# Layer norm, windowed attention and a gated unit on one core: the next chunk's rows are turned earlier, and other transfers change places

## The chip, the cores and the metric

The kernel runs on one core of a Trainium2 chip. A core has a matrix engine (TensorE, PE in the profile, with PEld for its weight loads), a vector engine (VectorE, DVE), a scalar engine (ScalarE, ACT), GpSimd (POOL) and a queue engine (SyncE, SP). Transfers between the chip's memory (DRAM) and the on-core memory are issued by an engine's queue, and run on 16 DMA engines that all queues share. The metric is the device time of one execution in microseconds; less is better.

## The reference

The input x has 2048 rows of 640 numbers. All numbers are bfloat16.

```python
xn = layernorm(x)                                  # rows: (x - mean) / sqrt(var + 1e-5)
q, k, v = split(xn @ wqkv)                         # 32 heads of 20 each
p = softmax(mask(q @ k.T * 20 ** -0.5))            # row i sees columns i-255 ... i
a = (p @ v) @ wo
b = (sigmoid(xn @ w_gate) * (xn @ w_up)) @ w_down  # 640 -> 1536 -> 640
out = x + a + b
```

`setup_inputs` also draws a `B_x`, which the reference does not use.

## The kernel before

The 2048 rows are worked in four chunks of 512 (c = 0 to 3), and each chunk in four blocks of 128 rows (s). Per chunk:

- **Rows.** `load_x` (L115) brings the chunk's x rows with four transfers into the tile `xc`, of which there is one buffer for all chunks. VectorE makes mean and variance of a block (`ln_block`, L214 and L220), POOL the inverse roots of all four blocks (`rstd_blocks`, L228 and L229), VectorE the normalized rows (`norm_rows`, L233). For chunks 1 to 3 the rows are then turned into columns in two halves: VectorE turns 32x32 squares (`turn_block`, L250), and `turn_rows` writes the result to DRAM with one transfer (L255) and reads it back in another order with four (L257) as `xnT`. Chunk 0 uses TensorE transposes instead.
- **Q and K.** `g_qk` has ten blocks of five matmuls (`proj_block`, L272): five of Q, copied out of PSUM by VectorE (L276), and five of K, copied by ScalarE (L278). Each copy is a tile `st`, one of six, which SP stores (L280) into a DRAM scratch, `sq` or `sk`. There a head has 32 rows, of which 20 are data; the other 12 are written once with zeros by `clear` (L153). `spread` (L290) reads the scratch back, one transfer for a pair of head groups, into `qT` and `kT`, where the scores read them. A chunk has four pairs (r = 0 to 3).
- **V.** `g_v` (L323): eight groups of ten short matmuls, copied by VectorE and ScalarE (L327).
- **Gate and up.** `g_gu` runs blocks of 128 of the 1536 hidden columns, twelve per chunk: five matmuls for the gate (L409), a tanh on ScalarE (L412), five matmuls for up (L416), and a product on VectorE (L420). The weights are loaded in eight transfers (`load_gu`, L156): the tiles `wg` and `wu` have two parts of 768 columns, each loaded in two halves of 384, so that a half serves three blocks.
- **Scores and P·V.** Chunk 0 has 16 score steps, the others 20. A step is 16 or 24 small matmuls (L492), one exponential on ScalarE (L498), masks on POOL (L481) and on VectorE (L509). Two steps after a pair's last score step its P·V follows (`pv`, L525), then VectorE turns and scales the result (L536 to L559).
- **Output.** `g_out`: down-projection (L430) and W_o (L437) into the same PSUM tile, VectorE adds x (L441), SP stores. `load_wd` (L176) loads W_down with five transfers; `turn_wo` (L185) reorders W_o in DRAM with eight transfers and `load_wo` (L190) loads the result.

The order of instructions on every engine is that of the program text; nothing is rescheduled. In front of the score steps and between them a queue of work called `fill` gives out matmul blocks: parts with names (`gu0a`, `gu0b`, `qk1`, `v1`, `gu0c`, and so on) that run in the order in which they were added, each with a cost in nanoseconds that says how much of it goes between two score steps. `mix(a, b, first, every)` takes a block of `a` and then a step of `b`, from block number `first` on. So steps for VectorE, such as statistics and turns, stand between the matmul blocks. Six half-blocks of gate and up run before the first score step; a chunk's first score step waits in the text for the whole of its `qk` part.

All matmul outputs but the scores go through four PSUM banks in rotation (`ps_d`); the scores have one tile of four banks. SP's transfers use eight semaphores in turn, so a transfer is issued once the eighth before it has landed.

Of the kernel before, what the change touches and what calls it, by code (L numbers as in the profile page):

```python
# [9 lines left out]
P = 128  # L10
# [5 lines left out]
DC = D // P  # L16
# [3 lines left out]
SBC = CW // P  # L20
# [5 lines left out]
FS = 768  # L26
# [10 lines left out]
FP32 = mybir.dt.float32  # L37
# [8 lines left out]
NP = NG // 2  # L46
# [20 lines left out]
def kernel(  # L67
# [11 lines left out]
    nc = tc.nc  # L79
    x2 = A_x.flatten_outer_dims()  # L80
# [3 lines left out]
    def pool(name, bufs, **kw):  # L84
        return ctx.enter_context(tc.tile_pool(name=name, bufs=bufs, **kw))
# [3 lines left out]
    lnp = pool("lnp", 4)  # L89
# [20 lines left out]
    def load_x(c):  # L110
        t = xp.tile([P, SBC, D], BF16, name="xc")
        xc[c] = t
        rows = x2[c * CW:(c + 1) * CW, :].rearrange("(a n t) d -> a t n d", a=SBC, n=SBC)
        for a in range(SBC):
            nc.sync.dma_start(out=t[32 * a:32 * a + 32], in_=rows[a])  # L115
# [3 lines left out]
    wg = [const.tile([P, DC, FS], BF16, name=f"wg{k}") for k in range(F // FS)]  # L119
    wu = [const.tile([P, DC, FS], BF16, name=f"wu{k}") for k in range(F // FS)]  # L120
# [30 lines left out]
    def clear(w):  # L151
        rows = scratch[w].rearrange("(h j) s -> h (j s)", j=32)[:, DH * CW:]
        nc.sync.dma_start(out=rows.rearrange("h (a e) -> h a e", a=4), in_=zero[:, 0:3, :])  # L153

    def load_gu(t, w, k, lo=0, hi=FS):
        nc.sync.dma_start(out=t[k][:, :, lo:hi],  # L156
                          in_=w.rearrange("(c p) f -> p c f", p=P)[:, :, k * FS + lo:k * FS + hi])

    load_gu(wg, B_w_gate, 0, 0, FS // 2)
    load_gu(wu, B_w_up, 0, 0, FS // 2)  # L160
    clear("q")
    clear("k")
    load_gu(wg, B_w_gate, 0, FS // 2)

    def load_rest():
        load_gu(wg, B_w_gate, 1, 0, FS // 2)
        load_gu(wu, B_w_up, 1, 0, FS // 2)
        load_gu(wg, B_w_gate, 1, FS // 2)
        load_gu(wu, B_w_up, 1, FS // 2)
        spread("q", 0, 2, NP)  # L170
        spread("k", 0, 2, NP)

    def load_wd():
        wd_r = B_w_down.rearrange("(c p) d -> p c d", p=P)
# [3 lines left out]
    wo_i = tc.dram_tile([HG, NG * DH, D], BF16, name="wo_i")  # L178
# [32 lines left out]
    def ln_half(c, s, a, stats=None):  # L211
        if a == 0:
            stats = lnp.tile([P, 2, nc.vector.BN_STATS_DIM], FP32, name="stats")
        nc.vector.bn_stats(out=stats[:, a, :], in_=xc[c][:, s, a * HALF:(a + 1) * HALF])  # L214
        return stats

    def ln_mv(stats, mv=None):
        if mv is None:
            mv = lnp.tile([P, nc.vector.BN_AGGR_DIM], FP32, name="mv")
        nc.vector.bn_aggr(out=mv, in_=stats)  # L220
        return mv

    def ln_block(c, s, mv=None):
        return ln_mv(ln_half(c, s, 1, ln_half(c, s, 0)), mv)

    def rstd_blocks(mvs):
        rstds = lnp.tile([P, SBC], FP32, name="rstds", bufs=1)
        nc.gpsimd.tensor_scalar(out=rstds, in0=mvs[:, :, 1], scalar1=EPS, scalar2=None, op0=ADD)  # L228
        nc.gpsimd.tensor_tensor(out=rstds, in0=rstds, in1=neghalf, op=POW)  # L229
        return rstds  # L230
# [13 lines left out]
    def turn_block(c, s):  # L244

        if s == 0:
            turns[c] = lnp.tile([P, SBC * D], BF16, name="turn", bufs=1)
        out_v = turns[c].rearrange("p (g m n t) -> p n g m t", g=HG, m=DC, n=SBC)
        in_v = xc[c][:, s, :].rearrange("p (m g j) -> p g m j", g=HG, m=DC)
        nc.vector.transpose(out=out_v[:, s], in_=in_v)  # L250

    def turn_rows(c):
        xnT[c] = xtp.tile([P, SBC, DC, P], BF16, name="xnT")
        rows = tc.dram_tile([HG, P, D], BF16, name=f"turn{c}")
        nc.sync.dma_start(out=rows.rearrange("g p e -> p g e"), in_=turns[c].rearrange("p (g e) -> p g e", g=HG))  # L255
        for g in range(HG):
            nc.sync.dma_start(out=xnT[c][32 * g:32 * g + 32].rearrange("p a m t -> p a (m t)"),  # L257
                              in_=rows[g].rearrange("(a j) e -> j a e", j=32))
# [3 lines left out]
    qk = {}  # L262
# [16 lines left out]
        dst = scratch[w].rearrange("(h j) s -> h j s", j=32)  # L279
        nc.sync.dma_start(out=dst[:, 4 * m:4 * m + 4, :], in_=st)  # L280

    def spread(w, c, r0, r1):

        half, first = divmod(r0, NP // 2)
        if first == 0:
            qk[w, c, half] = (qp if w == "q" else kp).tile([P, GH, CW], BF16, name=w + "T")
        src = scratch[w].rearrange("(a r p) s -> p r a s", a=2, p=P)
        to = qk[w, c, half].rearrange("p (r a) s -> p r a s", a=2)
        for r in range(r0, r1):
            nc.sync.dma_start(out=to[:, r % 2], in_=src[:, r])  # L290

    def new_v(c, s):
        v = vp.tile([P, 2, 16 * VW + 11], BF16, name="v")
# [35 lines left out]
    MM = 216  # L329

    def g_stats(c, out):


        mvs = lnp.tile([P, SBC, nc.vector.BN_AGGR_DIM], FP32, name="mvs", bufs=1)
        for s in range(SBC):
            ln_block(c, s, mvs[:, s, :])
            if s == SBC - 1:
                rstds = rstd_blocks(mvs)
            yield 0
        yield 0  # L340
        out.extend((mvs, rstds))

    def norm_rows(c, s, mvs, rstds):
        norm_block(c, s, mvs[:, s, :], rstds[:, s:s + 1], xc[c][:, s, :])
# [10 lines left out]
                turn_rows(c)  # L355
            yield 0

    def g_quick(c):
        got = []
        yield from g_stats(c, got)  # L360
        for s in range(0, SBC, 2):
            norm_rows(c, s, *got)
            norm_rows(c, s + 1, *got)
            yield 0
        for s in range(SBC):
            turn_block(c, s)
            if s == SBC - 1:
                turn_rows(c)
            yield 0

    def g_qk(c):
        for w in "qk":
            for m in range(DC):
                proj_block(w, c, m)
                if c == 0 and w == "q" and m == 1:
                    load_x(1)
                yield 5 * MM
        if c:
            spread("q", c, 0, 2)
            spread("k", c, 0, 2)  # L380
        else:
            for r in range(2):
                spread("q", c, r, r + 1)
                spread("k", c, r, r + 1)
                if r == 0:
                    load_gu(wu, B_w_up, 0, FS // 2)
# [14 lines left out]
    def part(w, d, f):  # L401
        k, first = divmod(f * P, FS)
        return w[k][:, d, first:first + P]

    def g_gu(c, f0, f1):
        for f in range(f0, f1):
            pg = ps_d.tile([P, CW], FP32, name="pg", tag="d")
            for d in range(DC):
                nc.tensor.matmul(pg, lhsT=part(wg, d, f), rhs=xnT[c][:, :, d, :],  # L409
                                 start=(d == 0), stop=(d == DC - 1))  # L410
            th = tp.tile([P, CW], FP32, name="th")
            nc.scalar.activation(out=th, in_=pg, func=TANH, scale=0.5)  # L412
            yield 5 * MM
            pu = ps_d.tile([P, CW], FP32, name="pu", tag="d")
            for d in range(DC):
                nc.tensor.matmul(pu, lhsT=part(wu, d, f), rhs=xnT[c][:, :, d, :],  # L416
                                 start=(d == 0), stop=(d == DC - 1))
            h = hp.tile([P, CW], BF16, name="h")
            ht[c, f] = h
            nc.vector.scalar_tensor_tensor(out=h, in0=th, scalar=1.0, in1=pu, op0=ADD, op1=MULT)  # L420
            yield 5 * MM
# [181 lines left out]
    def mix(a, b, first, every=1, rest=True):  # L603

        for k, cost in enumerate(a):
            yield cost
            if k >= first and (k - first) % every == 0:
                yield next(b, 0)
        if rest:
            yield from b  # L610
# [46 lines left out]
    r0 = root(mv0)  # L657
    r1 = root_act(1, xn1, neg1)
# [29 lines left out]
    nc.scalar.activation(out=scr, in_=neghalf[:, 0:1], func=EXP)  # L688
    banks.close()
    ps_s = banks.enter_context(tc.tile_pool(name="ps_s", bufs=1, space=bass.MemoryType.PSUM))  # L690
    for _ in g_qk(0):
        pass
    load_rest()

    fill = Fill()
    GU = 10 * MM
    OUT = 4 * 34 * 136
    APART = 1800
    def later(load, *args):
        load(*args)  # L700
        yield 0

    norms1 = g_quick(1)
    norms2 = itertools.chain(g_norms(2, True), later(load_x, 3))
    norms3 = g_norms(3, False)
    fill.add("gu0a", mix(g_gu(0, 0, 4), norms1, 0, 1, False), 4 * GU)
    fill.add("gu0b", mix(g_gu(0, 4, 10), norms1, 0), 6 * GU)
    fill.add("x2", later(load_x, 2), 0)
    fill.add("wo_i", later(turn_wo), 0)
    fill.add("qk1", g_qk(1), 50 * MM)  # L710
    fill.add("v1", mix(g_v(1), norms2, 2, 1, False), 40 * 136)
    fill.add("wd", later(load_wd), 0)
    fill.add("wo", later(load_wo), 0)
    fill.add("gu0c", mix(g_gu(0, 10, 12), norms2, 0, 1, False), 2 * GU)
    fill.add("gu1a", mix(g_gu(1, 0, 2), norms2, 0, 1, False), 2 * GU)
    fill.add("out0", mix(g_out(0, g_gu(1, 2, 3)), norms2, 1, 1), OUT + GU)
    fill.add("qk2", mix(g_qk(2), norms3, 2, 1, False), 50 * MM)
# [43 lines left out]
    c = NCH - 1  # L761
# [64 lines left out]
```

## Time and profile before

| | |
|---|---|
| median of three runs | 311.09 us (310.32 to 311.52) |
| the profiled execution | 311.1 us, its span 309.4 us |
| busy: PE, PEld, DVE, ACT, POOL | 303.5, 168.0, 187.2, 192.6, 79.1 us |
| granted TensorE clock | 1.00 throughout |
| moved by DMA | 36.86 MB, mean 119 GB/s |
| first Q matmul of chunk 0, of chunk 1 | 13.27 us, 51.27 us |
| first score step | 30.62 us |
| first matmul of the down-projection | 84.41 us |

The span is cut from the first to the last instruction of one profiled execution; its own time is 1.7 us longer. Times in the trace count from the start of the span. A row of a timeline has start, duration of the group, engine, line, operation, output and input, count, and in brackets the idle time before it with what ended it. For a transfer the row on a queue (SPq) is its issue; the time until its data has landed is a number of its own ("us to landing"). Busy times of PE overlap a little, since matmuls are pipelined, so a stall shows in the starts of the groups rather than in their sum.

### The profile page before, as it was taken

Reading aid. Unit: us, or ns where it says so; the run is one execution under the profiler, and the core shown is the slowest. Engines: PE = TensorE matmul, PEld = TensorE weight load, DVE = VectorE, ACT = ScalarE, POOL = GpSimd, SP = SyncE. Lnnn points to the kernel's source line nnn. Section 1 sums busy time; section 2 is a strip of 40 time slices with the busy share of each in tenths; the row PEclk is TensorE's granted clock in tenths of the full one; section 3 lists DMA queues with packets and bytes.
Section 4 is the critical chain, followed back from the end, with each engine's and each line's share of the span. In section 5 each row is a group of like instructions: output and inputs, shape, how many; then the busy total and the mean of one; then the engine's idle time right before and its main releaser. Section 6 shows DMA issues by size and latency. Waiting matters only on the chain.

```text
span 309.4 us, 10124 instructions
## 1 busy us (share of the span) xinstructions
PE 303.5 (98%) x4431; PEld 168.0 (54%) x4431; DVE 187.2 (61%) x372; ACT 192.6 (62%) x184; POOL 79.1 (26%) x172
## 2 busy tenths in 40 slices
PE   7999998999999999999999999999999999999996
PEld 3654443565456655644556655653445665444775
DVE  4736858659894679667653657346383627474423
ACT  6923875797674566869574656877676466768100
POOL 5000423133423123521223132331313232231100
PEclk9999999999999999999999999999999999999999
DMA  7987967549916722540251212560000110000301
GB/s 212 364 292 214 334 214 209 172 131 287 289 45 178 168 91 90 176 135 0 89 127 49 61 58 88 152 218 2 2 2 2 58 53 23 2 2 2 87 22 64
DMA packets 36140, 36.86 MB, mean 119 GB/s; under 512 B 2944, under 2 KB 35840, under 8 KB 36096
## 3 DMA queue, kind: packets, MB, share of 16 engines
q1 hardware_dynamic: 35232, 35.45, 37.7%
q10 hardware_dynamic: 864, 0.77, 0.9%
q8 instruction: 34, 0.56, 0.8%
q14 instruction: 10, 0.08, 0.1%
HBM read 25.59 MB, written 11.44 MB: 120 GB/s over the span
## 4 chain that ended last, share of the span: by engine, by line
PE 86%; DMA 4%; DVE 4%; issue 2%; ACT 1%; POOL 1%; SPq 1%; POOLq 0%; DVEq 0%
PE y L430 16%; PE pqk L272 15%; PE pu L416 14%; PE pg L409 13%; PE ps L492 8%; PE y L437 7%; PE pv L323 6%; PE acc L525 5%; DMA turn<-turn 2%; PE pv L303 1%; DMA xc<-in_A_x_dram 1%; ACT pT L498 1%; DMA xnT<-turn 1%; DVE h L420 1%; DVE stats L214 1%
## 5 line engine op out<-in xcount | busy, mean ns | idle before, releaser
L498 ACT ACTIVATE pT<-ps 128x2048 bf16<-128x2048 f32 x76 | 141.1, 1856 | 64.5 <-PE ps L492 56.9
L481 POOL TENSOR_SCALAR_AFFINE_SELECT pT<-pT 64x256 bf16<-64x256 bf16 (+1 forms) x120 | 68.1, 567 | 177.4 <-ACT pT L498 127.6
L409 PE MATMUL pg<-xnT,wg 128*128 128x512 bf16 x240 | 59.8, 380 | 0.0
L416 PE MATMUL pu<-xnT,wu 128*128 128x512 bf16 x240 | 59.8, 380 | 0.0
L430 PE MATMUL y<-wd,h 128*128 128x320 bf16 (+2 forms) x396 | 56.8, 295 | 0.0
L420 DVE SCALAR_TENSOR_TENSOR h<-th,pu 128x512 bf16<-128x512 f32 x48 | 32.6, 679 | 36.9 <-PE pu L416 18.9
L272 PE MATMUL pqk<-xnT,wqkv 128*128 128x512 bf16 x200 | 45.8, 381 | 1.3 <-DMA xnT<-turn 1.3
L430 PEld LDWEIGHTS <-h 128*128 128x128 bf16 x396 | 36.7, 98 | 16.2 <-issue 2.5
L509 DVE TENSOR_TENSOR pT<-pT,keep 128x512 bf16<-128x512 bf16 (+1 forms) x76 | 35.4, 468 | 11.5 <-ACT pT L498 10.5
L412 ACT ACTIVATE th<-pg 128x512 f32<-128x512 f32 x48 | 28.6, 595 | 15.5 <-PE pg L409 15.1
L416 PEld LDWEIGHTS <-wu 128*128 128x128 bf16 x240 | 22.0, 98 | 27.4 <-issue 2.7
L409 PEld LDWEIGHTS <-wg 128*128 128x128 bf16 x240 | 21.9, 98 | 27.0 <-issue 2.9
L272 PEld LDWEIGHTS <-wqkv 128*128 128x128 bf16 x200 | 22.4, 119 | 20.9 <-issue 3.5
L492 PE MATMUL ps<-qT,kT 20*64 20x320 bf16 (+4 forms) x1440 | 32.2, 260 | 0.1
L441 DVE SCALAR_TENSOR_TENSOR rows<-y,rows 128x320 bf16<-128x320 f32 x30 | 14.5, 490 | 27.0 <-PE y L437 24.6
L536 DVE STREAM_TRANSPOSE t<-acc 128x512 f32<-128x512 f32 x32 | 21.0, 695 | 13.6 <-PE acc L525 13.6
L492 PEld LDWEIGHTS <-kT 20*64 20x64 bf16 x1440 | 13.2, 103 | 23.4 <-issue 21.0
L437 PE MATMUL y<-wo,oc 128*128 128x320 bf16 (+2 forms) x165 | 24.2, 295 | 0.0
L525 PEld LDWEIGHTS <-v 64*32 64x32 bf16 x1440 | 17.1, 92 | 6.8 <-issue 1.8
L525 PE MATMUL acc<-pT,v 64*32 64x320 bf16 (+4 forms) x1440 | 20.3, 253 | 0.1
L437 PEld LDWEIGHTS <-oc 128*128 128x128 bf16 x165 | 15.6, 98 | 6.5 <-issue 0.8
L276 DVE CAST st<-pqk 128x512 bf16<-128x512 f32 x20 | 13.7, 686 | 7.4 <-PE pqk L272 7.2
(56 smaller groups left out, 173.6 us busy)
## 6 DMA issues: line engine op xcount, KB each, us to landing
qT<-sq SPq DMA_DIRECT2D x16, 256.0 KB, 4.5
kT<-sk SPq DMA_DIRECT2D x16, 256.0 KB, 4.8
xc<-in_A_x_dram SPq DMA_DIRECT2D x16, 160.0 KB, 4.2
sq<-st SPq DMA_DIRECT2D x20, 128.0 KB, 2.3
sk<-st SPq DMA_DIRECT2D x20, 128.0 KB, 2.1
out_dram<-rows SPq DMA_DIRECT2D x15, 160.0 KB, 1.8
wg<-in_B_w_gate_dram SPq DMA_DIRECT2D x4, 480.0 KB, 8.1
wu<-in_B_w_up_dram SPq DMA_DIRECT2D x4, 480.0 KB, 7.5
```

The source lines that it names most:

```text
L272: nc.tensor.matmul(ps, lhsT=wt[:, m, :], rhs=xnT[c][:, :, d, :], start=(d == 0), stop=(d == DC - 1))
L409: nc.tensor.matmul(pg, lhsT=part(wg, d, f), rhs=xnT[c][:, :, d, :], start=(d == 0), stop=(d == DC - 1))
L412: nc.scalar.activation(out=th, in_=pg, func=TANH, scale=0.5)
L416: nc.tensor.matmul(pu, lhsT=part(wu, d, f), rhs=xnT[c][:, :, d, :], start=(d == 0), stop=(d == DC - 1))
L420: nc.vector.scalar_tensor_tensor(out=h, in0=th, scalar=1.0, in1=pu, op0=ADD, op1=MULT)
L430: nc.tensor.matmul(y[:, 0:cut[1] - cut[0]], lhsT=ht[c, f][:, s * P:(s + 1) * P], rhs=wd[:, f, cut[0]:cut[1]], start=(f == 0), stop=False)
L437: nc.tensor.matmul(y[:, 0:cut[1] - cut[0]], lhsT=oc[c, m][:, s * P:(s + 1) * P], rhs=wo[:, m, cut[0]:cut[1]], start=False, stop=(m == DC - 1))
L481: nc.gpsimd.affine_select(out=part, in_=part, pattern=pattern, compare_op=GE, fill=0.0, base=-1 if sign > 0 else 0, channel_multiplier=sign)
L492: nc.tensor.matmul(ps[side * U:(side + 1) * U, i, col * U:(col + n) * U], lhsT=qk["k", kc, half][32 * i:32 * i + DH, 2 * r + side, kb * U: ...
L498: nc.scalar.activation(out=pt[:, :, 0:used, :], in_=ps[:, :, 0:used * U], func=EXP, scale=SCALE)
L509: nc.vector.tensor_tensor(out=part, in0=part, in1=limit.to_broadcast([P, HG, n * U]), op=MIN)
L525: nc.tensor.matmul(accs[side][32 * i:32 * i + 32, q * U:(q + n) * U], lhsT=vt[sb][rows, b, at:at + 32], rhs=pt[rows, i, col:col + n, :], s ...
```

## The change

It has five parts.

1. Chunk 1's rows are loaded ahead of the Q and K of chunk 0 instead of after Q's second block. Their statistics come behind the first four K blocks, the inverse roots behind the fourth. Their normalization and turning (`g_first`) stand behind the first six half-blocks of gate and up.
2. The two clears of the scratch move from ahead of Q to behind the third Q block and the first K block. The second half of the first gate part is loaded ahead of Q without the clears in front of it.
3. What `load_rest` issued behind Q and K is split: the first halves of the second weight part stay there, the second halves (`load_second`) move into chunk 1's Q, behind its third block. The spreads of pairs 2 and 3 of chunk 0 (`g_late`) move to behind half-blocks of gate and up 6 to 8, and are issued by POOL's queue.
4. Chunk 2's rows are loaded behind the first Q block of chunk 1, the reordering of W_o behind its first K block; both stood ahead of chunk 1's Q.
5. Nine blocks of gate and up run before chunk 1's Q, K and V instead of ten; three follow V instead of two, each half-block with one step of chunk 2's statistics and normalization.

```diff
 load_gu(wg, B_w_gate, 0, 0, FS // 2)
 load_gu(wu, B_w_up, 0, 0, FS // 2)
-clear("q")
-clear("k")
-load_gu(wg, B_w_gate, 0, FS // 2)
-
-def load_rest():
-    load_gu(wg, B_w_gate, 1, 0, FS // 2)
-    load_gu(wu, B_w_up, 1, 0, FS // 2)
+def load_second():
     load_gu(wg, B_w_gate, 1, FS // 2)
     load_gu(wu, B_w_up, 1, FS // 2)
-    spread("q", 0, 2, NP)
-    spread("k", 0, 2, NP)
...
-def spread(w, c, r0, r1):
+def spread(w, c, r0, r1, queue=nc.sync):
...
     for r in range(r0, r1):
-        nc.sync.dma_start(out=to[:, r % 2], in_=src[:, r])
+        queue.dma_start(out=to[:, r % 2], in_=src[:, r])
...
-def g_quick(c):
-    got = []
-    yield from g_stats(c, got)
+mvs1 = lnp.tile([P, SBC, nc.vector.BN_AGGR_DIM], FP32, name="mvs1", bufs=1)
+
+def g_first(rstds):
     for s in range(0, SBC, 2):
-        norm_rows(c, s, *got)
-        norm_rows(c, s + 1, *got)
+        norm_rows(1, s, mvs1, rstds)
+        norm_rows(1, s + 1, mvs1, rstds)
         yield 0
     for s in range(SBC):
-        turn_block(c, s)
+        turn_block(1, s)
         if s == SBC - 1:
-            turn_rows(c)
+            turn_rows(1)
         yield 0

-def g_qk(c):
+def g_late():
+    for r in range(2, NP):
+        for w in "qk":
+            spread(w, 0, r, r + 1, nc.gpsimd)
+            yield 0
+
+def g_qk(c, behind={}):
     for w in "qk":
         for m in range(DC):
             proj_block(w, c, m)
-            if c == 0 and w == "q" and m == 1:
-                load_x(1)
+            behind.get((w, m), lambda: None)()
             yield 5 * MM
...
-for _ in g_qk(0):
-    pass
-load_rest()
+load_x(1)
+load_gu(wg, B_w_gate, 0, FS // 2)
+for k, _ in enumerate(g_qk(0, {("q", 2): lambda: clear("q"), ("k", 0): lambda: clear("k")})):
+    if DC <= k < DC + SBC:
+        ln_block(1, k - DC, mvs1[:, k - DC, :])
+        if k == DC + SBC - 1:
+            rstds1 = rstd_blocks(mvs1)
+load_gu(wg, B_w_gate, 1, 0, FS // 2)
+load_gu(wu, B_w_up, 1, 0, FS // 2)
...
-norms1 = g_quick(1)
...
-fill.add("gu0a", mix(g_gu(0, 0, 4), norms1, 0, 1, False), 4 * GU)
-fill.add("gu0b", mix(g_gu(0, 4, 10), norms1, 0), 6 * GU)
-fill.add("x2", later(load_x, 2), 0)
-fill.add("wo_i", later(turn_wo), 0)
-fill.add("qk1", g_qk(1), 50 * MM)
+fill.add("gu0a", mix(g_gu(0, 0, 6), g_first(rstds1), 0), 6 * GU)
+fill.add("gu0b", mix(g_gu(0, 6, 9), g_late(), 1), 3 * GU)
+fill.add("qk1", g_qk(1, {("q", 0): lambda: load_x(2), ("q", 2): load_second, ("k", 0): turn_wo}), 50 * MM)
 fill.add("v1", mix(g_v(1), norms2, 2, 1, False), 40 * 136)
 fill.add("wd", later(load_wd), 0)
 fill.add("wo", later(load_wo), 0)
-fill.add("gu0c", mix(g_gu(0, 10, 12), norms2, 0, 1, False), 2 * GU)
+fill.add("gu0c", mix(g_gu(0, 9, 12), norms2, 0, 1, False), 3 * GU)
```

## The prediction

> **What bounds the kernel now.** I read the page first: which engine fills the span, and where the chain that ended last leaves it.
>
> ```profile
> span 309.4 us, 10124 instructions
> ...
> PE 303.5 (98%) x4431; PEld 168.0 (54%) x4431; DVE 187.2 (61%) x372; ACT 192.6 (62%) x184; POOL 79.1 (26%) x172
> ...
> L272 PE MATMUL pqk<-xnT,wqkv 128*128 128x512 bf16 x200 | 45.8, 381 | 1.3 <-DMA xnT<-turn 1.3
> ```
>
> PE is busy for 98% of the span and 86% of the chain lies on it. A change that leaves the number of matmuls alone, as this one does, can gain only where PE stands still. So next, the waits of PE, all of them:
>
> ```profile
> PE pqk L272 <- DMA xnT<-turn: 1.3, 1, 1.3
> PE pwarm L205 <- PEq L810: 0.8, 1, 0.8
> PE pt L239 <- DVE turn L642: 0.8, 1, 0.8
> ```
>
> The last two lie before 7 us and are not touched. The first is the wait for the turned rows of chunk 1. The chain of waits between 30 and 56 us shows who made it (columns: start, us, what):
>
> ```profile
> 30.98 0.24 POOL rstds L228
> ...
> 38.53 0.76 DVE turn L250
> ...
> 39.31 6.19 DMA turn<-turn
> ...
> 46.37 1.44 SPq L257
> ...
> 47.85 3.29 DMA xnT<-turn
> ...
> 51.27 2.33 PE pqk L272 x10
> ```
>
> The rows reach PE at 51.27; PE had run dry at 49.94. The write of the turned rows takes 6.19 us because SP's own timeline has 1.9 MB of weights and 1 MB of spreads issued just ahead of it:
>
> ```profile
> 30.19 1.13 SPq L156 DMA_DIRECT2D wg<-in_B_w_gate_dram  x1
> 31.36 2.54 SPq L156 DMA_DIRECT2D wu<-in_B_w_up_dram  x1
> 33.95 1.99 SPq L290 DMA_DIRECT2D qT<-sq  x2
> 35.99 1.13 SPq L290 DMA_DIRECT2D kT<-sk  x2
> 39.31 0.36 SPq L255 DMA_DIRECT2D turn<-turn  x1
> ```
>
> Cut into single microseconds, the windows show 310 to 373 GB/s from 29 to 43 us, nearly nothing from 43 to 46. Last, a stall that a busy PE hides: the weight loads of the P·V of chunk 0's last pair.
>
> ```profile
> 82.72 0.10 PEld L525 LDWEIGHTS <-v 64*32 64x32 bf16 x4 [0.42 <-ACT pT L498]
> 83.11 0.88 PEld L525 LDWEIGHTS <-v 64*32 64x32 bf16 x68 [0.29 <-DVE h L420]
> ```
>
> These 72 matmuls take 1.40 us; the same 72 took 1.03 at 44.75 and at 71.33. Their second bank is freed by VectorE's h of 82.37 to 83.05: 0.37 us lost.
>
> **The change part by part**
>
> *Rows of chunk 1 early (gain).* Their load moves from 16.95 to right behind the first weights. It waits until VectorE has read chunk 0's last block out of the same buffer (10.07 + 0.45 = 10.52), and SP stands from about 8.4 till then. Queued behind are half a gate weight (used at 30.98) and the first Q store (15.26): free. With the rows, 4.75 MB are queued; 13 us at 274 GB/s leave 1.2 MB, 3.4 us at the 350 of the next windows, so they land at about 16.4 + 2 = 18.4. VectorE is free at 19.55, behind Q's five copies, and had then idled 3.35 us. Four blocks at 0.88 + 0.21 end at 23.9, POOL's root (0.23 + 1.04 and handoffs) at 25.4. Then, between the h's, four normalizations (1.87 in all) and four turns at 0.82: done at about 32.6, not 39.29.
>
> *Turned rows (gain).* Ahead of the write stand four spreads and three weights from 25.49 on: 2.5 MB, of which 0.6 move before 29 us; the rest needs 5.6 us at 340 GB/s, the rows 1.9 more: 36.5, plus 2.3 (now the stream stops at 43.2 and the write counts as landed at 45.50): 38.8. From there to the last rows took 5.6 us (45.52 to 51.14): 44.4 at the latest. Q now starts a block earlier, at 47.16. 2.8 us of cover: the wait of 1.33 goes. The block itself is only moved behind V.
>
> *Clears.* Their issues (2.01 and 0.59) now lie between stores: a store 0.53 and a clear 0.59 against a copy every 1.08, nothing. But the first K spread waits for K's clear and the last K store, now until 27.09, and the first scores run at 30.62, 3.5 us later, where the shortest landing of such a spread is 3.3. So the cover is 0.2 us. Issued at about 21.2, the clear would land at 23.3 by a store's 2.1, and at 29.4 by its own 8.2 of before: 0 to 2.1 us. I take 0: the 8.2 fell where the windows show 274 to 416 GB/s, now it falls where DMA share goes from 0.92 to 0.37, and the rows of chunk 1 are out of the way.
>
> *Late spreads, on POOL's queue.* Four leave SP (3.1 us of issue there, free) and stand between POOL's masks. The trace has no DMA issued by POOL. Call its cost d. Nearest rows: SP issues the same spread in 0.36 to 1.42 us, any transfer in at most 2.01. I take 1.0, and keep 0.4 and 2.0. The first runs in POOL's gap from 40.5 to 44.67. K's and the next Q's come behind the masks that end at 45.91, then masks of 1.53, another spread, masks of 1.06: these end at 48.5 + 3d, or 51.9 if ScalarE is the later. The P·V that reads them is at 58.76, after the change 57.4: free up to d = 2.95. Pair 2's scores (56.12, then 54.8) need the spread issued at 45.91 + d, landing in 3.3 to 8.2: at most 56.1, at 1.0 and the median 4.8 it is 51.7.
>
> *SP behind it.* The first Q store of chunk 1 overwrites what the spreads read, so SP waits for them: 45.91 + 2d + 3.3 = 51.2. Behind wait ten stores (0.53 each), chunk 2's rows (1.85), two weights (1.0) and the eight turns of W_o (5.1): 13.3 us, the last K store out at 64.5; and since SP's transfers take eight semaphores in turn, the fourth W_o turn waits until the gate weight issued at 54.6 lands. At 340 GB/s that is near 60, so 65.5; by the median 8.1, 68. Now it is 66.52. From there run the spreads, then W_down, whose last part lands at 75.1 + 9.0 = 84.1 and is used at 85.8. With PE 1.7 earlier, that store may end at 66.5. I take 65.5: nothing; kept end +1.5.
>
> *VectorE behind V.* One more gate block there brings two statistics steps forward and uses 0.62 us in which VectorE now waits. Adding its rows up from the first statistics (65.7), h of chunk 1's first block ends at 79.9, and the P·V wants the bank at 81.2. The 0.37 goes; kept end: it stays.
>
> **Sum.** The profiled execution took 311.1 (span 309.4 and 1.7 around it), the median is 311.09, so the one stands for the other. 311.1 − 1.33 − 0.37 = 309.4 us, −0.55%. About 0.5% (1.55 us) is what a measurement of this kernel can tell from no change.
>
> [...]
>
> **Rivals**
>
> 1. *Slower: POOL's queue.* From d = 2.95 P·V waits for masks at 3 us per us of d; SP's stores slip by 2 per us, and W_down with them. P·V is late by 3(d − 2.95), W_down by 2d + 62.5 − 66.5 even without the landing of a weight. At d = 3.0 that is 2 us, above the old time; over 0.5% slower needs 3.3 us given back, d = 3.65; at 4 it is 313.4. For it: no row shows a DMA on POOL, VectorE is busy 62, 67 and 59% in 40 to 50, 50 to 55 and 55 to 60 us. Against: the largest issue on SP is 2.01, and POOL is busy 26% of the span. [...]
> 2. *SP late, at small d.* K's clear (up to 2.1) or the weight ahead of W_o's turns (up to 1.5) gives back 0.5 to 2.5: 309.9 to 311.9. For it: the covers of 0.2 and 1.0. Against: the clear's new place, and a DMA share of 0.21 and less from 43 to 46.
> 3. *Only the row wait goes:* 309.8. VectorE is 93% busy from 72 to 80, and my sum of its rows may be 1.4 us off.
> 4. *The change does not do what it says:* rows land late and the wait stays, 310.7 to 311.1. It takes 2.8 us; counted with 2.
>
> **How the numbers follow.** Both waits gone 0.50; rival 3 0.13; rival 2 with 4 0.20; rival 1 0.17. The predicted time is the likeliest's, 309.4, its own range 308.9 to 309.8. The first case ends beyond −0.5% nearly always, 0.46, and rival 3 in 0.02: faster 0.48. Rival 1 is slower in 0.16, rival 2 in 0.02: slower 0.18. The rest, 0.34, is within 0.5%. Range 308.8 to 312.4: down to both gains and 0.6 for what repeated runs differ by (310.32 to 311.52), up through rivals 2 and 3 and the foot of 1.
>
> **What would show it.** Right: no PE wait for xnT; turned rows issued near 32.6 on SP and landed by 44.4; first Q matmul of chunk 1 near 47.2; first scores still near 30.6; P·V of pair 3 in 1.03 us; last K store of chunk 1 out by 66. Wrong: POOL DMA rows above 2 us each with P·V waiting for POOL; PE waiting for kT near 30.6; PE waiting for wd after 82.

## The result, and the profile after

The changed kernel takes 313.75 us (median of 20 runs, 311.10 to 316.48); beside it the kernel before takes 310.98 (20 runs). The ratio is 1.0075, with an interval of 1.0048 to 1.0102: slower, by 0.75%, where 309.4 was forecast (ratios leave out runs more than 1.5% above a kernel's fastest, so they can differ from the ratio of the medians). The median lies above the range of 308.8 to 312.4. In 13 of the 20 runs the mean granted clock is 0.993 to 0.995 and the time 313.5 to 316.5; in the other 7 the clock is 0.998 or more and the time 311.1 to 312.3. The profiled run (313.88 us) is one of the 13.

The page first, its span and its engines:

```profile
span 312.2 us, 10134 instructions
...
PE 305.0 (98%) x4431; PEld 168.1 (54%) x4431; DVE 187.5 (60%) x372; ACT 192.3 (62%) x184; POOL 82.3 (26%) x176
```

PE is busy for 1.5 us more with the same 4431 matmuls, so something made matmuls longer; in the rest of the 2.8 us PE stood. The waits of PE name it:

```profile
PE y L428 <- DMA wd<-in_B_w_down_dram: 1.7, 1, 1.7
...
PE y L428 <- DVE h L418: 0.5, 1, 0.5
```

The wait for the turned rows (1.3 before) is gone. In its place stands one for W_down, and a small one for VectorE. Next the timeline of PE (start, duration, what, and in brackets the wait):

```profile
46.94 1.24 PE L265 MATMUL pqk<-xnT,wqkv 128*128 128x512 bf16 x5
...
81.14 1.03 PE L523 MATMUL acc<-pT,v 64*32 64x320 bf16 x72
...
82.46 1.84 PE L428 MATMUL y<-wd,h 128*128 128x320 bf16 x10
85.97 1.49 PE L428 MATMUL y<-wd,h 128*128 128x320 bf16 x8 [1.67 <-DMA wd<-in_B_w_down_dram]
87.39 0.65 PE L490 MATMUL ps<-qT,kT 20*64 20x256 bf16 x16
87.97 1.78 PE L428 MATMUL y<-wd,h 128*128 128x320 bf16 x6
```

The first three rows are the forecast come true: Q of chunk 1 starts at 46.94, pair 3's P·V takes 1.03 us, and the down-projection is reached at 82.46, where before it was 84.41. The kernel is 1.95 us ahead here. Then ten of the 18 matmuls run, and PE stands until 85.97. What follows is slow: six down-projection matmuls took 0.99 us before and take 1.78 now. The windows of single microseconds say why (columns: stretch, length, busy time and count of PE, PEld, DVE, ACT and POOL, the granted clock, the DMA share, GB/s):

```profile
83.00:84.00 1.00, 0.85 (x7) 0.48 (x5) 1.00 (x3) 1.00 (x1) 0.00 (x0) 1.00 1.12 234
84.00:85.00 1.00, 0.30 (x2) 0.10 (x1) 0.96 (x3) 0.48 (x1) 0.46 (x1) 1.00 1.15 198
85.00:86.00 1.00, 0.04 (x1) 0.04 (x1) 1.00 (x3) 0.00 (x0) 0.58 (x2) 1.00 1.07 207
86.00:87.00 1.00, 1.00 (x8) 0.64 (x7) 1.00 (x2) 0.00 (x0) 0.00 (x0) 0.91 0.70 156
87.00:88.00 1.00, 1.00 (x19) 0.23 (x18) 1.00 (x4) 0.00 (x0) 0.00 (x0) 0.50 0.22 55
...
90.00:91.00 1.00, 1.00 (x5) 0.32 (x3) 0.43 (x1) 0.05 (x1) 0.00 (x0) 0.88 1.01 364
```

PE is idle for 1.8 us from 83.8 on (by the starts of its matmuls the standstill is 2.1), and from 86.82 to 90.24 the clock is halved. That is 3.41 us (a clock of 0.91 over one us is 0.18 us at half; then three whole us; 0.88 is 0.24 us at half). The chain of waits leads back from the standstill (start, us, what):

```profile
70.71 4.59 DMA qT<-sq
...
75.32 10.60 DMA wd<-in_B_w_down_dram
...
85.97 1.49 PE y L428 x8
```

So the question is why SP got to W_down late. SP's own timeline of after, and below it that of before:

```profile
50.45 0.52 SPq L273 DMA_DIRECT2D sq<-st  x1
51.02 2.06 SPq L115 DMA_DIRECT2D xc<-in_A_x_dram  x4
...
54.40 0.62 SPq L156 DMA_DIRECT2D wg<-in_B_w_gate_dram  x1
55.07 0.56 SPq L156 DMA_DIRECT2D wu<-in_B_w_up_dram  x1
...
58.46 6.19 SPq L178 DMA_DIRECT2D wo_i<-in_A_wo_dram  x8
64.75 2.52 SPq L273 DMA_DIRECT2D sk<-st  x4
...
72.77 2.97 SPq L169 DMA_DIRECT2D wd<-in_B_w_down_dram  x5
```

```profile
50.56 5.11 SPq L185 DMA_DIRECT2D wo_i<-in_A_wo_dram  x8
55.78 3.85 SPq L280 DMA_DIRECT2D sq<-st  x5
59.73 6.79 SPq L280 DMA_DIRECT2D sk<-st  x5
...
71.17 4.62 SPq L176 DMA_DIRECT2D wd<-in_B_w_down_dram  x5
```

Before, W_o's eight turns are out of SP before the first Q store. Now they stand between K's first store and its other four, behind x rows and two weights. From the first Q store (50.45) to the end of the last K store (67.27) SP takes 16.8 us, and its first W_down issue comes 1.60 us later than before (72.77 against 71.17), though PE needs W_down 1.95 sooner. Of the 1.60, 0.70 is there when the spreads begin (67.32 against 66.62); 0.90 is added among the eight spreads, one of which takes 1.25 to issue where the same one took 0.36 before. The last part of W_down is issued at 75.32, once the spread of 70.71 has landed, and lands at 85.92.

The account by the starts of PE's steps, after minus before: −1.94 at score step 17, just ahead of the down-projection; 1.63 behind it at step 19; 2.43 at PE's last matmul. Standstill and half clock took 3.57 together. Of the last 0.8, 0.7 went between 157 and 172 us, where the second row of the waits (0.5) lies. The other 0.35 of the 2.8 lies behind PE's last matmul: from its end to the end of the span 3.02 us pass (309.15 to 312.17), and 2.67 before (306.71 to 309.38).

### The profile page after: what moved, and what is told of

Read it like the earlier page. It is cut to its first block, busy times and chain, and to the rows that moved or that the text cites. A ratio compares the mean times of both kernels' runs of the same rounds, so it can differ in the third digit from the quotient of the medians.

```text
span 312.2 us, 10134 instructions
## 1 busy us (share of the span) xinstructions
PE 305.0 (98%) x4431; PEld 168.1 (54%) x4431; DVE 187.5 (60%) x372; ACT 192.3 (62%) x184; POOL 82.3 (26%) x176
## 4 chain that ended last, share of the span: by engine, by line
PE 89%; DMA 6%; ACT 2%; DVE 2%; issue 1%; POOL 0%; SPq 0%; DVEq 0%; POOLq 0%
PE y L428 17%; PE pu L414 16%; PE pg L407 15%; PE pqk L265 14%; PE ps L490 8%; PE y L435 7%; PE acc L523 6%; PE pv L316 5%; DMA wd<-in_B_w_down_dram 3%; DMA qT<-sq 1%; PE pv L296 1%; ACT pT L496 1%; DMA xc<-in_A_x_dram 1%; PE pvh L296 0%; DVE h L418 0%
## 5 line engine op out<-in xcount | busy, mean ns | idle before, releaser
L428 PE MATMUL y<-wd,h 128*128 128x320 bf16 (+2 forms) x396 | 58.0, 299 | 2.3 <-DMA wd<-in_B_w_down_dram 1.7
L410 ACT ACTIVATE th<-pg 128x512 f32<-128x512 f32 x48 | 28.6, 595 | 16.8 <-PE pg L407 16.5
L549 DVE TENSOR_TENSOR on<-t,rec 128x320 bf16<-128x320 f32 x32 | 17.5, 586 | 0.6
```

Source lines behind the costliest of these rows:

```text
L428: nc.tensor.matmul(y[:, 0:cut[1] - cut[0]], lhsT=ht[c, f][:, s * P:(s + 1) * P], rhs=wd[:, f, cut[0]:cut[1]], start=(f == 0), stop=False)
```

## The experiments

Two theories stood at the start. Theory A: SP is one queue in series; W_o's turns ahead of K's stores delay the spreads and W_down behind them. Theory B: the POOL queue or the bytes of the late spreads did it. Later a third question came up, the order of PE's work.

**W_o's turns put back ahead of Q**, all else as changed:

```diff
-    fill.add("qk1", g_qk(1, {("q", 0): lambda: load_x(2), ("q", 2): load_second, ("k", 0): turn_wo}), 50 * MM)
+    fill.add("wo_i", later(turn_wo), 0)
+    fill.add("qk1", g_qk(1, {("q", 0): lambda: load_x(2), ("q", 2): load_second}), 50 * MM)
```

> The changed kernel with the eight turns of W_o issued ahead of chunk 1's Q, in SP's idle stretch from 42.6 to 50.4 us, instead of behind the first K block. Nothing else moves, PE's order is that of the changed kernel. Theory A (the loss is the wait for the last part of W_down, because SP's issues of the W_o turns stand between the K stores and the spreads; 2.1 us of standstill, and the half clock of 3.4 us that follows it): the K stores go out with their copies, near 62, W_down is issued 4 us sooner, the wait and the half clock are gone; 0.7 us that PE loses near 160 us stays: 309.9 us, clock 1.00. Rival B (the landing of W_down is set by the bytes queued ahead of it, not by when SP issues it): W_down lands near 85.5 again, the time is that of the changed kernel, 311.5 to 314.

Measured: 310.81 us (12 runs), ratio 0.9975 (0.9959 to 0.9991), 0.998 or more of the clock in every run. SP issues W_down from 68.03 instead of 72.77, the last part lands at 82.2, and the wait for it is gone from the list of PE's waits, where now stand, behind those of the head:

```profile
PE y L428 <- DVE h L418: 0.5, 1, 0.5
PE ps L490 <- ACT pT L496: 0.3, 1, 0.3
```

With this one line moved, the wait and the half clock are gone. The changed kernel itself did not run beside it; the kernel of the next experiment, which differs from it by one line, did (ratio 1.0009), and a later pair on one chip changes the place of W_o alone. The gain is 0.5 us where the sum had 1.7, and 309.9 was expected: two waits remain.

**The late spreads on SP instead of POOL**, all else as changed, on two chips:

```diff
-                spread(w, 0, r, r + 1, nc.gpsimd)
+                spread(w, 0, r, r + 1)
```

> The changed kernel with the four late spreads on SP's queue instead of POOL's; same place in the text. Theory A: SP is idle when they come, the first Q store still waits for its copy and for their landing near 50, so the W_down wait stays: 311.5 to 314 us, as the changed kernel. Rival C (POOL's queue is what costs: its spreads delay the masks or the stores): the time falls by 1.5 us or more.

> The changed kernel with the four late spreads on SP's queue, now beside the changed kernel on one chip. Before, it came out at 311.7 on another chip, with SP's own times as in the changed kernel. Theory A (POOL's queue has no part, the difference was the chip): within 0.5% of the changed kernel here, 313 to 314.5. Rival C (POOL's spreads make something late): 1.5 us or more below it.

> The changed kernel itself, as the yardstick for the three beside it on one chip: 311.1 to 316.5 us, median near 313.7, the half clock in some two runs of three, PE waiting some 2 us for the last part of W_down.

Measured: on the first chip 311.74 us, ratio 1.0009 (0.9985 to 1.0033), with no wait for W_down in the profile, but 0.9 of the scores for ScalarE; on the second 313.02, ratio 1.0059 (1.0035 to 1.0082), with a wait for W_down of 1.0 us in the profile. The changed kernel beside it on the second chip took 312.20, ratio 1.0039 (1.0026 to 1.0052), with 2.4 us of that wait in the profile. In this set of runs its loss is 0.4%, and the clock is 0.993 in one of its six runs; a median near 313.7 and the half clock in two runs of three were expected. The intervals of its two sets just touch (1.0048 and 1.0052). The POOL queue does not make the wait: without it the wait can still be there, and the time is no better on the one chip where both ran. It has a small price of its own all the same, at the end of the program. From the end of PE's last matmul to the end of the span the eight profiles with spreads on POOL take 3.02 or 3.03 us, the six without 2.66 to 2.68. On POOL itself the changed kernel's timeline shows

```profile
40.45 0.94 POOL L283 DMA_DIRECT2D qT<-sq  x1
...
46.32 0.72 POOL L283 DMA_DIRECT2D qT<-sq  x1
```

and 0.73 for each of the other two. VectorE, whose load rival 1 had named in its favour, was busy for 2.43 of the 3.12 us that the four issues took; none came near the 2.95 from which that rival costs time.

**W_down ahead of V in `fill`**, so that its five issues come before the four last spreads of chunk 1 (71.81 and 76.30 in the profile):

```diff
-    fill.add("v1", mix(g_v(1), norms2, 2, 1, False), 40 * 136)
     fill.add("wd", later(load_wd), 0)
+    fill.add("v1", mix(g_v(1), norms2, 2, 1, False), 40 * 136)
```

> The changed kernel with W_down's five loads issued ahead of the last four spreads of chunk 1 instead of behind them; the W_o turns stay between the K stores. Theory A (what PE waits for is W_down's place in the queue): its last part is issued 2 us sooner and lands by 83.5, PE's wait at the down-projection falls from 2.1 to at most 0.3 us, the clock stays at 1.00: 310.5 to 311.3 us, as with the W_o turns early. Rival B (the bytes of this stretch set it, whatever their order): the wait only moves to the scores that need the last spreads, 313 to 314.

Measured: 311.79 us, ratio 1.0030 (1.0012 to 1.0047). No wait for W_down (its last part landed at 83.51 and was used after 85.17), but 0.9 us of the scores' wait for ScalarE, and the 0.5 for VectorE. The expectation of 310.5 to 311.3 is missed by half a microsecond. Between score step 7 and the last matmul the profile loses 1.4 us: 1.0 up to step 13, with the scores' wait in it, and 0.8 near 160, less the 0.37 of pair 3's P·V. This profile also loses clock ahead of anything that the edit touches: its mean is 0.994, and ten of chunk 0's V matmuls take 2.80 us from 7.19 on, where the same ten take 1.60 in the changed kernel; all later starts are 1.9 us later than in the changed kernel. Taking the W_down wait away is not enough.

**The first two parts alone** (rows and clears early; weights, spreads, W_o and blocks as before):

```diff
-    for _ in g_qk(0):
-        pass
+    load_x(1)
+    load_gu(wg, B_w_gate, 0, FS // 2)
+    for k, _ in enumerate(g_qk(0, {("q", 2): lambda: clear("q"), ("k", 0): lambda: clear("k")})):
+        if DC <= k < DC + SBC:
+            ln_block(1, k - DC, mvs1[:, k - DC, :])
...
-    fill.add("gu0b", mix(g_gu(0, 4, 10), norms1, 0), 6 * GU)
+    fill.add("gu0b", g_gu(0, 4, 10), 6 * GU)
```

> The kernel before with parts 1 and 2 alone: chunk 1's rows loaded, normalized and turned early, the clears between the stores; all weights and spreads stay ahead of the turned rows, ten blocks ahead of chunk 1's Q. Theory A (the rows wait for the 1.9 MB of weights and 1 MB of spreads ahead of them): SP reaches the write of the turned rows at 37.2, but it lands near 45 as before, so PE still waits about 1 us: 310.5 to 311.1 us. Rival E (the late normalization was what held the rows): the wait is gone, 309.5 to 309.8.

Measured: 310.93 us, ratio 1.0011 (0.9995 to 1.0026): nothing, as expected. PE waits 1.2 us at the same place as before. The profile puts this wait down to a mask on VectorE, but PE goes on at 51.33, behind the last rows. On SP:

```profile
30.35 1.48 SPq L156 DMA_DIRECT2D wg<-in_B_w_gate_dram  x1
...
33.45 2.11 SPq L286 DMA_DIRECT2D qT<-sq  x2
...
36.83 0.42 SPq L251 DMA_DIRECT2D turn<-turn  x1
45.01 1.75 SPq L253 DMA_DIRECT2D xnT<-turn  x4
```

The turned rows wait in the queue behind weights and spreads, and their write, issued 2.48 us sooner than before (36.83 against 39.31), takes 8.2 us to land instead of 6.19; the last rows land at 51.20, as late as before (51.14). In the changed kernel, with two of those weights and four of those spreads moved away as in part 3, the write landed at 39.51 and the last rows at 45.5: the early rows are worth something only where the bytes ahead of them are moved too.

**The last part alone** (nine and three blocks, in the kernel before):

```diff
-    fill.add("gu0b", mix(g_gu(0, 4, 10), norms1, 0), 6 * GU)
+    fill.add("gu0b", mix(g_gu(0, 4, 9), norms1, 0), 5 * GU)
...
-    fill.add("gu0c", mix(g_gu(0, 10, 12), norms2, 0, 1, False), 2 * GU)
+    fill.add("gu0c", mix(g_gu(0, 9, 12), norms2, 0, 1, False), 3 * GU)
```

> The kernel before with part 5 alone: nine blocks of gate and up ahead of chunk 1's Q, K and V, three behind. The turned rows come when they came, so PE's wait for them grows by that block, from 1.33 to 3.7 us. Theory A with the clock: the granted clock falls to a half for some 3.4 us behind a standstill of this length, 1.7 us more, and the changed order near 160 us 0.7: 314 to 316 us, clock 0.995. Rival D (the half clock belongs to something else in the changed kernel, the standstill alone has no such price): 313.5 to 314 us at clock 1.00.

Measured: 318.18 us, ratio 1.0212 (1.0179 to 1.0246), more than was expected. The wait for the rows grows by the block that no longer covers it, from 1.3 to 4.0 us, and its windows show the clock:

```profile
50.00:51.00 1.00, 0.00 (x0) 0.01 (x1) 0.00 (x0) 0.00 (x0) 0.00 (x0) 0.76 1.08 222
51.00:54.00 3.00, 2.98 (x22) 0.94 (x23) 0.64 (x2) 0.00 (x0) 0.00 (x0) 0.50 0.89 195
...
57.00:58.00 1.00, 1.00 (x6) 0.44 (x4) 0.07 (x1) 0.00 (x0) 0.00 (x0) 0.83 0.00 0
```

Half clock from 50.52 to 57.34: 6.82 us, twice 3.41. PE's last matmul is 6.3 us late: 2.7 of longer wait, 2.8 to 3.4 of half clock (PE was standing in its first 0.5), a new wait of 0.5 at 66.0, where Q and K's matmuls wait for VectorE, and 0.8 in the stretch near 160 us, as in the changed kernel, less the 0.37 of pair 3's P·V and a head that is 0.3 shorter. So the block count costs time of its own, without any of the other parts.

**W_o early, second weight halves early, ten and two blocks as before.** The halves of `load_second` go out behind the turned rows, so that none stands among the Q stores:

```diff
-    fill.add("gu0b", mix(g_gu(0, 6, 9), g_late(), 1), 3 * GU)
+    fill.add("second", later(load_second), 0)
+    fill.add("gu0b", mix(g_gu(0, 6, 10), g_late(), 1), 4 * GU)
+    fill.add("wo_i", later(turn_wo), 0)
...
-    fill.add("gu0c", mix(g_gu(0, 9, 12), norms2, 0, 1, False), 3 * GU)
+    fill.add("gu0c", mix(g_gu(0, 10, 12), norms2, 0, 1, False), 2 * GU)
```

> As e1, with ten blocks ahead of chunk 1's Q and two behind V, so that PE's order is that of the kernel before in every place; the second weight halves are issued behind the turned rows. Theory A: no wait for the rows, none for W_down; the 0.7 us near 160 us, which come from the order, are gone too, but the 0.37 us at the P·V of chunk 0's last pair may stay: 309.2 to 309.6 us, clock 1.00. If the order has no part in it, e5 is at e1's time or 0.4 above.

> The kernel with W_o's turns ahead of Q, the second weight halves ahead of the gate blocks, and ten and two blocks as before, once more, beside three neighbours that differ from it by one thing each. Theory A (one queue in series, and the order of PE's work): no wait for W_down, no wait of the scores for ScalarE at step 11, shift against before -1.8 us from step 7 to the end: 309.2 to 309.8 us on a chip where the kernel before takes 311.0. Rival B (its earlier 309.7 was chance of that chip): 310.3 to 311.0.

Measured: 309.71 us, ratio 0.9946 (0.9927 to 0.9966), and on another chip 310.34, ratio 0.9968 (0.9946 to 0.9989). PE's order is now that of before, and its lead stays, in the first profile, at 1.77 us from score step 7 to the last matmul (304.95 against 306.71). All of PE's waits but those of the head are gone. Pair 3's P·V takes 1.40 us again, as before: that 0.37 was a gain of the nine blocks. Its second set lies above the 309.2 to 309.8 that was expected; in that profile the lead is 1.48 at step 7 and 1.18 at the end, 0.2 of the loss at the down-projection.

Three neighbours of it ran beside that second set, on the same chip, each with one thing changed.

**Nine and three blocks** in it, to price PE's order by itself:

```diff
-    fill.add("gu0b", mix(g_gu(0, 6, 10), g_late(), 1), 4 * GU)
+    fill.add("gu0b", mix(g_gu(0, 6, 9), g_late(), 1), 3 * GU)
...
-    fill.add("gu0c", mix(g_gu(0, 10, 12), norms2, 0, 1, False), 2 * GU)
+    fill.add("gu0c", mix(g_gu(0, 9, 12), norms2, 0, 1, False), 3 * GU)
```

> The same as the one with ten and two blocks, but with nine and three, as in the change. Tells the order of PE's work from the late landing of Q's stores. Theory A: the second halves are out of the Q stores' way, so the 0.3 us wait of the scores for ScalarE near step 11 is gone, but the order of blocks and scores differs from before in 25 places and the 0.75 us near 160 us stay: 310.1 to 310.6, which is 0.5 to 0.9 above the neighbour. Rival C (the order costs nothing by itself, the 0.75 us came from late stores): equal to the neighbour within 0.3 us, 309.4 to 310.0.

Measured: 310.73 us, ratio 0.9982 (0.9964 to 0.9999); 0.39 above its neighbour by the medians, 0.71 by PE's last matmul in the profiles (306.24 against 305.53). 310.1 to 310.6 was expected, 0.5 to 0.9 above the neighbour. The scores' wait for ScalarE, which the kernel with only W_o early had, is gone. There the last K copy on ScalarE stood 0.90 us for an `st` tile that a Q store still held, and the exponential behind it was late; so the weights among the Q stores made that wait. That this place gets cheaper without them is not shown, for at 59.23 another wait has come up, the one that the last part alone had too:

```profile
PE pqk L265 <- DVE t L534: 0.6, 1, 0.6
```

The copy on ScalarE, in ScalarE's timeline of the kernel with only W_o early:

```profile
62.28 0.59 ACT L271 CAST st<-pqk 128x512 bf16<-128x512 f32 x1 [0.90 <-DMA sq<-st]
62.76 1.88 ACT L496 ACTIVATE pT<-ps 128x2048 bf16<-128x2048 f32 x1
```

The wait for VectorE near 160 us stays in this kernel. On PE, and then on VectorE:

```profile
154.40 1.67 PE L428 MATMUL y<-wd,h 128*128 128x320 bf16 x11
156.58 1.94 PE L428 MATMUL y<-wd,h 128*128 128x320 bf16 x13 [0.51 <-DVE h L418]
```

```profile
154.19 1.29 DVE L557 STREAM_TRANSPOSE oc<-on 128x512 bf16<-128x512 bf16 x2
155.41 0.51 DVE L507 TENSOR_TENSOR pT<-pT,keep 128x768 bf16<-128x768 bf16 x1
155.85 0.67 DVE L418 SCALAR_TENSOR_TENSOR h<-th,pu 128x512 bf16<-128x512 f32 x1
```

One block more behind V changes what stands between score steps in 27 further places, the last of them ahead of score step 65 (the steps count from 0 to 75). In one of them two turns and a mask of VectorE come just ahead of the h that the down-projection needs next.

**The late spreads on SP** in it (the one-line edit shown above):

> The neighbour with ten and two blocks and W_o early, but with the late spreads issued by SP instead of POOL. Theory A: POOL's queue has no part in gain or loss; SP has 3 us to spare before the first Q store of chunk 1: equal to the neighbour within 0.3 us, 309.3 to 310.0, no wait for W_down. Rival D (the POOL queue is needed, SP is short by the four issues): turned rows or Q stores of chunk 1 about 2 to 3 us later, a wait for W_down or the turned rows, 310.5 or more.

Measured: 309.46 us, ratio 0.9936 (0.9910 to 0.9961), no wait of PE outside the head; PE's last matmul 1.64 us ahead of before. It is the fastest of all, and POOL's queue is not needed. That it lies 0.9 below its neighbour was not expected. In the one pair of profiles 0.2 of that is there by score step 1, 0.2 comes near 84 us, and 0.36 lies behind the last matmul: 2.67 to the end of the span against 3.03, the price of POOL's queue seen above. Only this last part can be laid to the edit.

**W_o's turns behind the first K block** in it, their place in the change:

```diff
-    fill.add("wo_i", later(turn_wo), 0)
-    fill.add("qk1", g_qk(1, {("q", 0): lambda: load_x(2)}), 50 * MM)
+    fill.add("qk1", g_qk(1, {("q", 0): lambda: load_x(2), ("k", 0): turn_wo}), 50 * MM)
```

> The neighbour with ten and two blocks, but with W_o's turns back behind the first K block, as in the change; second weight halves stay ahead of the gate blocks. The place of W_o alone. Theory A (SP in series from the first Q store of chunk 1): the last K store goes out at about 65.5 to 66.5, W_down is issued from about 71.5, its last part lands at 84 to 85.5, and PE at 82.5 waits for it 0.5 to 2 us, with the half clock in some runs: 310.3 to 312 us. Rival E (the weights between the Q stores were the harm, W_o's place is free): no wait for W_down, 309.4 to 310.0.

Measured: 314.04 us (310.43 to 318.00; 310.3 to 312 was expected), ratio 1.0044 (1.0009 to 1.0078); by the ratios 0.8% (2.4 us) above the neighbour that differs in this alone, by the medians 3.7 us. The profiled run is one of its two longest (317.93), so its waits are more than the usual. SP's timeline, the wait, and the windows:

```profile
59.32 6.37 SPq L178 DMA_DIRECT2D wo_i<-in_A_wo_dram  x8
65.79 2.52 SPq L273 DMA_DIRECT2D sk<-st  x4
...
74.68 5.05 SPq L169 DMA_DIRECT2D wd<-in_B_w_down_dram  x5
```

```profile
PE y L428 <- DMA wd<-in_B_w_down_dram: 4.1, 5, 1.3
```

```profile
85.00:86.00 1.00, 0.24 (x2) 0.04 (x1) 0.96 (x3) 0.00 (x0) 0.69 (x2) 0.74 1.09 225
86.00:90.00 4.00, 1.99 (x7) 0.88 (x7) 3.90 (x8) 0.00 (x0) 0.00 (x0) 0.50 0.82 162
...
95.00:96.00 1.00, 1.00 (x11) 0.23 (x17) 0.49 (x1) 0.00 (x0) 0.00 (x0) 0.64 0.00 0
```

PE waits five times, for each part of W_down, and the clock is halved from 85.49 to 95.73: 10.24 us, three times 3.41. There are no weights among the Q stores here, so it is W_o's place that makes the wait.

## Why the prediction was wrong

Point by point, by its own steps:

- *Rows of chunk 1 early, turned rows:* right. The write was issued at 32.05 (32.6 forecast) and landed at 39.51 (38.8); the last rows landed at 45.5, 1.1 later than "44.4 at the latest", still ahead of their use at 46.94. The wait of 1.33 went.
- *Clears:* right. K's clear was issued at 21.19 and landed in 4.2 us; the first K spread landed at 29.70, the first scores ran at 30.40. The cover of 0.2 that was given was 0.7.
- *Late spreads, on POOL's queue:* right for the issue. d was 0.72 to 0.94, 1.0 was taken; rival 1 (break-even at 2.95) fell. But the 0.35 us that the queue adds behind the last matmul was in no term.
- *VectorE behind V:* right for the 0.37 in pair 3's P·V; and incomplete, see below.
- *SP behind it:* this step failed. "13.3 us, the last K store out at 64.5", then "I take 65.5: nothing". Measured from the first Q store, which came at 50.45 (51.2 forecast), the ten stores, the rows, the weights and W_o's turns took 16.8 us, 3.5 more. The ten stores cost 6.3 instead of 5.3 (one took 0.95, and the groups hold gaps), the rows 2.06 instead of 1.85, the weights 1.23 instead of 1.0, the turns 6.19 instead of 5.1 (one took 1.55), and the gaps between these groups, which were counted at nothing, 1.0. The wait for a weight's semaphore, the reason for 65.5, came to 0.2 at 61.2. The last K store was out at 67.27, beyond the 66.5 that the step itself named as its limit.
- *"75.1 + 9.0 = 84.1 and is used at 85.8":* the same step's cover at W_down was too large as well. The last issue moved by only 0.2, to 75.32, but its part took 10.60 to land and came 1.8 later than 84.1. The 9.0 is the median of three landings that the trace of before has (8.87, 8.97 and 9.60, parts 2 to 4; those of the first and the last part are missing), and the last part takes longest: after the change the five took 6.85, 7.69, 8.42, 9.33 and 10.60. Parts 2 to 4 landed 0.42 to 0.74 later than before, the first W_o load behind W_down 0.85 later. By an estimate from these (85.92 less 0.65 to 0.85) the last part landed at 85.1 to 85.3 before, 0.5 to 0.7 ahead of its use and not 1.7. So of the 2.1 us of standstill most is PE's own lead of 1.95 meeting a thin cover, and 0.65 to 0.85 is later landing. This is rival 2, for W_o's turns, priced at 0.5 to 2.5 with a chance of 0.20 (with rival 4).
- *No price for PE's clock.* No term of the sum, and none of the rivals, had the half clock after a standstill. It turned rival 2's 2 us into 3.57, and put the median above its bound of 311.9. Without it, in the 7 runs at full clock, the kernel is at 311.1 to 312.3, with a median of 311.5, still no faster than before.
- *"The block itself is only moved behind V":* wrong in size. It moved PE's order in 27 places after it, and cost about 0.8 us near 160, as three kernels with nine blocks show (this one, the last part alone, and the neighbour).

So the forecast gain was real and appears at 82.46 us; what failed is the step "SP behind it", the belief that SP had slack of 1.0 us where it was 0.8 us short, in front of a load that had less cover than was taken.

## What to carry to other kernels

When a step is moved on a queue, add up the queue from its first release to the first issue that somebody waits for, with the gaps between issues and with the landings (here 6.85 us for the first part of W_down and 10.60 for the fifth), and compare it with the need as the change will make it, not as it was: here PE came 1.95 us sooner to a load that was issued 1.60 later. Give a standstill of PE a second price for the clock where the traces have shown one: here 1.81 us of idle PE within 3.41 were followed by 3.41 us at half clock, and 1.33 by none. A part that looks like a mere shift in a queue of filler work changes all the places after it; keep the order of the bound engine and move only transfers, and bring in no further queue without need, as the kernel at 309.46 does.

## What was not expected of the hardware

The half clock comes in pieces of one length: 3.41 us in the changed kernel, 6.82 with the block alone, 10.24 with W_o behind K and ten blocks, which is once, twice and three times 3.41. In the changed kernel's trace it starts at 86.82, ends at 90.24, and comes back behind the last matmul, at 312.10: 221.86 us later, 65 times 3.413.

How much PE was busy in the 3.41 us ahead of each of the three falls of the clock, and, for the kernel before, in 3.41 us that hold the whole of its wait for the rows:

| kernel | stretch, us | PE busy in it, us of 3.41 | clock behind it |
|---|---|---|---|
| the last part alone | 47.10 to 50.52 | 0.00 | 0.50 |
| changed | 83.41 to 86.82 | 1.60 | 0.50 |
| W_o behind K, ten blocks | 82.08 to 85.49 | 1.83 | 0.50 |
| before | 49.90 to 53.31 | 2.08 | 1.00 |

So PE was idle for all of the stretch in one case only; in the other two the fall came behind 1.81 and 1.58 us of idle PE, and the 1.33 us of the kernel before cost no clock in its profile. That is read off single profiles, in which the ends of matmuls are modelled, and no run varied the standstill alone: from what length on it costs clock is not shown. On the second chip the changed kernel's two waits for W_down (2.4 us) came with a mean clock of 0.993 in the profiled run, and the one wait with the spreads on SP (1.0 us) with 1.000. Nor does the clock fall at once: PE's last matmul ends at 309.15 in the changed kernel and the fall comes 2.95 us later; in the kernel before the clock is still 1.00 when the span ends, 2.67 us after the last matmul. Ahead of each return to full clock PE was busy throughout: 1.00 of every us from 87 to 90 in the changed kernel, 3.00 of the 3 us from 54 to 57 with the block alone, 3.00 of the 3 from 92 to 95 with W_o behind K.

One kernel need not pay each time: the mean clock of the changed kernel is 0.993 to 0.995 in 13 runs of 20 in one set and 0.993 in 1 of 6 in another, and that of the kernel before is 0.995 and 0.994 in two of the 30 runs beside W_o behind K (313.42 and 313.46 us). What made the difference is not shown, since all but the profiled runs have no trace. W_down ahead of V shows a place in the head where clock can go.
